# Decode kernel with two attention and two gated layers: the last normalisation from a scaled copy of x, rows of x by 32x32 transposition on VectorE, addition to x moved behind

## The chip, the core and the metric

One core of a Trainium2 chip runs the kernel. The metric is the device time of one execution in microseconds (us); three runs of the kernel before gave a median of 313.3 us. The core's engines are TensorE (PE, with its weight loads shown apart as PEld), VectorE (DVE), ScalarE (ACT), GpSimd (POOL) and SyncE (SP). Each takes its instructions in the order of the program; between engines they wait on semaphores.

## What is computed

Four rows of 512 numbers (one token for each of four sequences) pass through attention with a cache, a gated layer, the same attention again and the same gated layer again. Each of the four adds to x, and each starts with a normalisation of x.

```python
def _layernorm(x, axis=-1, eps=1e-5):
    m = jnp.mean(x, axis=axis, keepdims=True)
    v = jnp.var(x, axis=axis, keepdims=True)
    return (x - m) / jnp.sqrt(v + eps)
...
    def _A_ref(x, k_cache, v_cache, wq, wo):    # B=4, Sq=1, D=512, 32 heads, 8 kv heads, 4096 keys of 128
        q = (x @ wq).reshape(B, Sq, Hq, Dh).transpose(0, 2, 1, 3)
        scores = jnp.einsum("bhqd,bhkd->bhqk", q, k) * (Dh ** -0.5)
        p = _softmax(scores, axis=-1)
        o = jnp.einsum("bhqk,bhkd->bhqd", p, v)
        return o.transpose(0, 2, 1, 3).reshape(B, Sq, Hq * Dh) @ wo
...
    def _B_ref(x, w_gate, w_up, w_down):        # 512 -> 1792 -> 512
        g = jnp.einsum("bsd,df->bsf", x, w_gate)
        u = jnp.einsum("bsd,df->bsf", x, w_up)
        h = _sigmoid(g) * u
        return jnp.einsum("bsf,fd->bsd", h, w_down)
...
    x = x + _A_ref(_layernorm(x, axis=-1), A_k_cache, A_v_cache, A_wq, A_wo)
    x = x + _B_ref(_layernorm(x, axis=-1), B_w_gate, B_w_up, B_w_down)
    x = x + _A_ref(_layernorm(x, axis=-1), A_k_cache, A_v_cache, A_wq, A_wo)
    x = x + _B_ref(_layernorm(x, axis=-1), B_w_gate, B_w_up, B_w_down)
```

## The kernel before

Nearly all of the kernel is the two attention layers: 32 pairs of sequence and key-value head in each, whose keys and values stream from memory in 1 MB tiles and are worked on in an order written out by hand (`ORDER`, `LOADS`, `PROGRAM`). The change touches none of that. It touches the end, from line 1446 on: the last piece of attention's output projection, the last normalisation and the last gated layer.

The helper class `_Sched` keeps one list of instructions for each engine. `S.group`, `S.inst`, `dve(...)` and `act(...)` append to them in the order of the source; `reads` and `writes` are names of values, from which the waits follow, those between two instructions of one engine included. So the order of two statements in the source is the order of the queue when both go to one engine.

x lies transposed in `xT`: 128 partitions, 4 groups k of columns, 4 sequences b, so 16 numbers per partition. The end of the kernel before runs as follows; the line numbers are those of the profile.

- `do_wo` and `wo_units` (lines 1282 to 1321): the output projection of a head adds to `xT`: matmuls of line 1299 into a bank `O_ps`, then the addition on VectorE, line 1313. The last call of `do_wo` has a `then`, which is run between the two: `mean_of_last` (line 615).
- Mean: `mean_before` (605) sums x as it stands before the last addition, in two bf16 parts (`parts`, lines 588 and 589); `mean_of_last` (621) adds what the last addition will bring. Both sum into `M_ps[1]`.
- `ident_w` (1463, ScalarE) is a float32 identity, `eye4` (1465, VectorE) a small selection matrix made from it.
- `ln_a` (486): `xc_sb` = x minus mean (508, VectorE), `xc_bf`, its bf16 form times a constant (524, ScalarE), and the squares `sq_sb` (529, VectorE).
- Rows of x: eight float32 matmuls of line 1477 against `ident_w` turn `xT` into rows in bank `S_ps[1]` (the trace has them as 16), and line 1490 copies them to `x_row` (ScalarE). Row group c, at partitions 32c to 32c+3, holds the 128 columns c of x for the four sequences.
- `parts` splits the squares in two bf16 parts; `gate(0, 2)` issues the first 8 of the gate's 56 matmuls (744); `square_sums_of_parts` (634) sums the squares with two matmuls; `ln_b` (643) makes from them the reciprocal root `rs`, by nine small instructions on VectorE one after the other (648, 655, 660, then 558, 563, 569 twice); `gate(2, KF)` issues the other 48 matmuls, multiplies the gate by `rs` (757, VectorE) and takes the tanh (767, ScalarE).
- `sel_row` and `rowk_f` (1493, 1498, VectorE): `rs` as a scalar for each partition.
- `up_half(0)` and `up_half(1)`: 28 matmuls each (778), and on VectorE (788) the product with the gate, which gives the two halves of `hT_bf`.
- Down projection (1509): 56 matmuls in two groups; the first needs the first half of `hT_bf`, the second the second. Four go to four row groups of the bank at a time.
- Line 1522 (VectorE) multiplies by `rowk_f` and adds `x_row`; four DMAs (1531) write the four row groups out.

The order of TensorE's queue at the end is therefore 1299, 621, 1477, 744 (8), 634, 744 (48), 778 (28), 778 (28), 1509 (56).

Of the kernel before, what the change touches and what calls it, by code (L numbers as in the profile page):

```python
# [146 lines left out]
def bass_interleave_layers__gqa_block_cached__glu_gated_glu__decode_kernel(  # L147
# [17 lines left out]
    P = 128  # L165
# [98 lines left out]
    sq_sb = t_row[:, D // 2 + KD * Bn:D // 2 + 2 * KD * Bn].rearrange("p (k b) -> p k b", k=KD)  # L264
    ident_f = t_row[:, 0:P]
    half_f = t_row[:, P:P + 8 * REP].rearrange("p (u w) -> p u w", u=2)
    gs_sb = t_row[:, 0:KF * Bn]
    t_sb = t_row[:, 64:64 + KF * Bn]
    iota_f = pe_sb.rearrange("p j m -> p (j m)").bitcast(dt.float32)[:, 0:P]
# [213 lines left out]
    def bc(ap2, n, nb):  # L483
        return ap2.unsqueeze(1).broadcast_to([P, n, nb])
# [116 lines left out]
    def mean_before():  # L601
        S.group(
            "pe",
            [
                (lambda n, k: lambda e: e.matmul(
                    M_ps[1][:, 0:Bn], lhsT=ones_wb, rhs=sq_hl[:, n, k * Bn:(k + 1) * Bn],
                    start=(n == 0 and k == 0), stop=False,
                ))(n, k)
                for n in range(2) for k in range(KD)
            ],  # L610
            reads=["rb", "ones_b"],
            writes=["M1"],
        )

    def mean_of_last(us):
        u = seq[NU - 1][2]
        assert us == [u]
        S.last_write["M1"] = S.group(
            "pe",
            [  # L620
                (lambda n, r: lambda e: e.matmul(
                    M_ps[1][:, 0:Bn], lhsT=ws_hl[:, n, r:r + 1].broadcast_to([P, P]),
                    rhs=oT_sb[:, u * REP + r, 0:Bn], start=False, stop=(n == 1 and r == REP - 1),
                ))(n, r)
                for n in range(2) for r in range(REP)
            ],
            reads=["wsb"] + [f"oT_{u}_{c}" for c in range(Bn)],
        )
# [11 lines left out]
            writes=["M1"],  # L640
        )

    def ln_b(nb, sums=square_sums):
        M = M_ps[1]
        if sums is not None:
            sums(nb)
        dve(
            lambda e: e.tensor_reduce(
                lnsq[:, 0:nb], M[:, 32:32 + KD * nb].rearrange("p (k b) -> p b k", k=KD), AX.X, ALU.add
            ),  # L650
            reads=["M1"],
            writes=["nt_b"],
        )
        dve(
            lambda e: e.tensor_scalar(vpe[:, 0:nb], lnsq[:, 0:nb], inv_d, eps, op0=ALU.mult, op1=ALU.add),
            reads=["nt_b"],
            writes=["vpe"],
        )
        dve(
            lambda e: e.tensor_scalar(  # L660
                y0i[:, 0:nb], vpe[:, 0:nb].bitcast(dt.int32), -0.5, RSQRT_MAGIC, op0=ALU.mult, op1=ALU.add
            ),
            reads=["vpe"],
            writes=["y0i"],
        )
        y0 = y0i[:, 0:nb].bitcast(dt.float32)
        if nb == 1:
            newton_one(y0)
        else:
            newton_many(y0, nb)  # L670
# [552 lines left out]
    def normalise(g, uls=(0, 1)):  # L1223
        l, b, u = seq[2 * g]
        bank, key = out_of(g, uls[0])
        c = b if l == 1 else own_column
        u0, n = u + uls[0], len(uls)
        for ul in uls:
            assert not any(t[0] == l and t[2] == u + ul for t in ready)
            done.add((l, b, u + ul))  # L1230
            if l == 0 or all((1, bb, u + ul) in done for bb in range(Bn)):
                ready.append((l, b, u + ul))
        dve(
            lambda e: e.tensor_tensor(  # L1234
                oT_sb[:, u0 * REP:(u0 + n) * REP, c],
                bank[:, uls[0] * REP:(uls[0] + n) * REP],
                rden_sb[:, uls[0] * REP:(uls[0] + n) * REP],
                ALU.mult,
            ),
            reads=[key, "rden"],  # L1240
            writes=[f"oT_{u + ul}_{c}" for ul in uls],
        )
# [39 lines left out]
    def wo_units(us, l, b, p, then=None):  # L1282
        if l == 0:
            assert len(us) == 2
            if rows_in[b] < HKV // 2 - 1:
                wo_rows(us, b)
                return
            assert turning == [b, 3]
            turning.clear()
        bs = range(Bn) if l == 1 else [b]  # L1290
        cs = range(Bn) if l == 1 else [own_column]
        nb = len(bs)
        n = REP * len(us)
        out_w = O_ps[p][:, 64:64 + KD * nb]
        fns = []
        for c in range(KD):
            for r in range(n):
                fns.append(
                    (lambda c, r: lambda e: e.matmul(  # L1299
                        out_w[:, c * nb:(c + 1) * nb],  # L1300
                        lhsT=wo_sb[:, us[0] * REP + r, cols(c)],
                        rhs=oT_sb[:, us[0] * REP + r, cs[0]:cs[0] + nb],
                        start=(r == 0),
                        stop=(r == n - 1),
                    ))(c, r)
                )
        S.group(
            "pe", fns, reads=[f"oT_{u}_{c}" for u in us for c in cs] + [f"wo{u}" for u in us], writes=[f"O{p}"]
        )
        if then is not None:  # L1310
            then(us)
        dve(
            lambda e: e.tensor_tensor(
                xT[:, :, bs[0]:bs[0] + nb],
                xT[:, :, bs[0]:bs[0] + nb],
                out_w.rearrange("p (k b) -> p k b", k=KD),
                ALU.add,
            ),
            reads=[f"O{p}"],
            writes=[f"x{bb}" for bb in bs],  # L1320
        )

    def do_wo(p, then=None):
        if not ready:
            return False
        l, b, u = ready.pop(0)
        us = [u]
        if u % 2 == 0 and (l, b, u + 1) in ready:
            ready.remove((l, b, u + 1))
            us.append(u + 1)  # L1330
        wo_units(us, l, b, p, then)
        return True
# [114 lines left out]
        pass  # L1447
    parts(sq_hl, xT.rearrange("p k b -> p (k b)"), xkeys, "rb")
    mean_before()
    normalise(g, (1,))  # L1450
    do_wo((g + 1) % 2, mean_of_last)
    assert not ready
    free += spare
    assert not loads and len(free) == NSLOT + KD
# [1 line left out]
    home = free[0]  # L1456
    assert home not in free[-2:]
    ident_w = slot[home][:, 0:2 * P].bitcast(dt.float32)
    x_row = slot[home][:, 2 * P:4 * P].bitcast(dt.float32)
    eye4 = slot[home][:, 4 * P:4 * P + 2 * Bn].bitcast(dt.float32)  # L1460
    sel_row = slot[home][:, 4 * P + 16:4 * P + 16 + 2 * Bn].bitcast(dt.float32)
    o_row = slot[home][:, 5 * P:6 * P]
    act(lambda e: e.activation(ident_w, ident_bf[:, :], ACTF.Copy), reads=IDENT, writes=[f"s{home}"])
    dve(
        lambda e: e.tensor_reduce(
# [2 lines left out]
        reads=[f"s{home}"],  # L1468
        writes=["eye4"],
    )  # L1470

    ln_a(0, Bn, 0.5 * RS, M_ps[1][:, 0:Bn])
    fns = []
    for c in range(KD):
        for e_ in range(2):
            fns.append(
                (lambda c, e_: lambda e: e.matmul(
                    S_ps[1][32 * c:32 * c + Bn, bass.ds(e_, P // 2, step=2)],
                    lhsT=xT[:, c // 2 * 2 + e_, :],
                    rhs=ident_w[:, P // 2 * (c % 2):P // 2 * (c % 2 + 1)],  # L1480
                    start=True,
                    stop=True,
                ))(c, e_)
            )
    S.group("pe", fns, reads=xkeys + [f"s{home}"], writes=["S1"])
    parts(sq_hl, sq_sb.rearrange("p k b -> p (k b)"), ["rd"], "rb")
    gate(0, 2)
    square_sums_of_parts()
    ln_b(Bn, None)
    act(lambda e: e.activation(x_row, S_ps[1][:, 0:P], ACTF.Copy), reads=["S1"], writes=["x_row"])  # L1490
    gate(2, KF)
    dve(
        lambda e: e.tensor_tensor(sel_row, eye4, rs, ALU.mult),
        reads=["eye4", "rs"],
# [4 lines left out]
        reads=["sel_row"],  # L1499
        writes=["rowk"],  # L1500
    )
    up_half(0)
    up_half(1)
    for part in range(2):
        fns = []
        for k in range(KW * part, KW * part + KW):
            for c in range(KD):
                fns.append(
                    (lambda c, k: lambda e: e.matmul(
                        S_ps[0][32 * c:32 * c + Bn, 0:P],  # L1510
                        lhsT=hT_bf[:, k, :],
                        rhs=wd_sb[:, k, c * P:(c + 1) * P],
                        start=(k == 0),
                        stop=(k == KF - 1),
                    ))(c, k)
                )
        if part == 0:
            S.group("pe", fns, reads=["rc"] + wkeys["wd"], writes=["S0"])
        else:
            S.last_write["S0"] = S.group("pe", fns, reads=["rc", "rd"] + wkeys["wd"])  # L1520
# [8 lines left out]
        S.dma(  # L1529
            ("sp", "act")[c % 2],  # L1530
            (lambda c: lambda e: e.dma_start(
                out.rearrange("b s d -> (b s) d")[:, c * P:(c + 1) * P], o_row[32 * c:32 * c + Bn, :]
            ))(c),
            f"out{c}",
            reads=["o_row"],
# [47 lines left out]
```

## Time and profile before

| | us |
|---|---|
| median of three runs | 313.3 (312.93 to 313.76) |
| profiled execution, its time | 312.81 |
| span of its records | 310.6 |
| TensorE busy | 227.0 (73%) |
| VectorE busy | 179.8 (58%) |
| ScalarE busy | 106.8 (34%) |
| GpSimd busy | 40.4 (13%) |
| end of the last VectorE instruction (1522) | 308.31 |

The span is divided below into start times within it. The memory queues are busy to about the 296th microsecond; what lies behind is the tail that the change edits. In each stretch of that tail the profile has the same granted TensorE clock, 0.50 of full speed. A timeline line reads: start, time, engine, line, operation, what it writes and reads, its shape and how often; in square brackets the engine's idle time before it and what ended it.

### The profile page before, as it was taken

To read this page: it belongs to the slowest core of one execution; us is meant where nothing else is said; L and a number is where in the kernel's file an instruction comes from. 1 tells how busy PE (TensorE), PEld (TensorE's weight loads), DVE (VectorE), ACT (ScalarE), POOL (GpSimd) and SP (SyncE) were. 2 spreads that over 40 slices of the span, in tenths; PEclk is the share of its full clock that TensorE was granted. 3 is DMA by queue.
4 is the path that set the end of the run, shared out by engine and by line. 5 is a ranking of instruction groups with operands and counts; after the bars stand their busy time and mean duration, and the time that the engine had idled before them with its cause. 6 is when DMAs were issued, how large, how long until landed. Compare 5 with 4: busy or idle time off the path is not lost.

```text
span 310.6 us, 10146 instructions
## 1 busy us (share of the span) xinstructions
PE 227.0 (73%) x4306; PEld 138.5 (45%) x4306; DVE 179.8 (58%) x395; ACT 106.8 (34%) x351; POOL 40.4 (13%) x205
## 2 busy tenths in 40 slices
PE   1232366244889789799879898986768989789975
PEld 1220133032654354646444664544533754446765
DVE  6364757406334757587652468775565793894333
ACT  2010124204303365434234625236424313445600
POOL 0011110200000213011112011021101110212000
PEclk9999999999999855667755557575555575755555
DMA  7999999999999999999999999999999999999900
GB/s 290 417 424 411 407 422 378 390 406 419 407 415 418 413 379 415 426 418 418 419 390 386 424 421 420 421 419 419 420 414 424 400 358 401 424 422 420 407 27 5
DMA packets 20788, 120.45 MB, mean 388 GB/s; under 512 B 1924, under 2 KB 6024, under 8 KB 7688
## 3 DMA queue, kind: packets, MB, share of 16 engines
q1 hardware_dynamic: 20720, 119.81, 94.9%
q8 instruction: 34, 0.56, 0.7%
q14 instruction: 10, 0.08, 0.1%
q10 hardware_dynamic: 24, 0.01, 0.0%
HBM read 119.80 MB, written 0.00 MB: 386 GB/s over the span
## 4 chain that ended last, share of the span: by engine, by line
PE 26%; DMA 16%; DVE 9%; issue 4%; ACT 4%; POOL 1%; DVEq 0%; ACTq 0%; POOLq 0%; SPq 0%
DMA slot<-in_A_k_cache_dram 9%; PE O_ps L1203 8%; DMA slot<-in_A_v_cache_dram 7%; PE S_ps L1034 6%; DVE slot L1017 6%; PE PT L1105 3%; ACT pT L1157 3%; PE O_ps L1299 2%; PE M_ps L907 1%; POOL qz L731 1%; ACT pe L1083 1%; DVE small L1052 1%; PE O_ps L1060 1%; PE AC L1259 1%; PE M_ps L956 1%
## 5 line engine op out<-in xcount | busy, mean ns | idle before, releaser
L1017 DVE STREAM_TRANSPOSE slot<-slot 128x2048 f32<-128x2048 f32 (+1 forms) x50 | 101.5, 2040 | 24.5 <-DMA slot<-in_A_k_cache_dram 24.5
L1157 ACT ACTIVATE pT<-PT 32x128 bf16<-32x128 f32 x236 | 63.1, 267 | 58.6 <-PE PT L1105 38.6
L1034 PE MATMUL S_ps<-slot,qz 128*16 128x512 bf16 x496 | 56.6, 586 | 22.0 <-DVE slot L1017 10.9
L1203 PEld LDWEIGHTS O_ps<-pT,slot 128*128 128x128 bf16 x1856 | 54.8, 103 | 32.0 <-ACT pT L1157 19.2
L1203 PE MATMUL O_ps<-pT,slot 128*128 128x4 bf16 x1856 | 58.2, 166 | 12.3 <-ACT pT L1157 7.2
L1083 ACT ACTIVATE pe<-S_ps,small 128x512 bf16<-128x512 f32 x32 | 22.0, 687 | 71.6 <-DVE small L1071 41.2
L731 POOL COPY qz<-qs 32x32 bf16<-32x32 bf16 x128 | 26.0, 203 | 106.2 <-PE S_ps L1034 62.8
L1052 DVE TENSOR_REDUCE small<-S_ps 128x1 bf16<-128x512 f32 x32 | 21.9, 684 | 29.1 <-PE S_ps L1034 28.8
L1034 PEld LDWEIGHTS S_ps<-slot,qz 128*16 128x16 bf16 x496 | 10.6, 102 | 40.6 <-DVE slot L1017 13.2
L1105 PE MATMUL PT<-ident_bf,pe 128*128 128x64 bf16 (+1 forms) x288 | 27.7, 235 | 1.1 <-ACT pe L1083 1.0
L1105 PEld LDWEIGHTS PT<-ident_bf,pe 128*128 128x128 bf16 (+1 forms) x288 | 20.3, 123 | 13.6 <-ACT pe L1083 3.9
L1071 DVE CUSTOM_DVE_ANT_0 O_ps<-O_ps,small 128x64 f32<-128x64 f32 x32 | 9.0, 282 | 20.2 <-PE O_ps L1060 11.6
L1116 POOL CAST small<-small 128x1 bf16<-128x1 f32 x32 | 5.9, 186 | 99.7 <-ACT pe L1083 76.8
L1259 PE MATMUL AC<-wo,oT 128*1 128x512 bf16 x96 | 12.1, 617 | 7.5 <-DMA wo<-in_A_wo_dram 7.0
L907 PE MATMUL M_ps<-wq,small 128*1 128x512 bf16 x128 | 14.6, 604 | 0.0
L1060 PE MATMUL O_ps<-valid_p,small 128*128 128x64 bf16 x32 | 7.1, 223 | 8.5 <-DVE small L1052 8.5
L1234 DVE TENSOR_TENSOR oT<-O_ps,small 128x8 bf16<-128x8 f32 (+1 forms) x32 | 5.3, 164 | 13.3 <-PE O_ps L1203 12.6
L1060 PEld LDWEIGHTS O_ps<-valid_p,small 128*128 128x128 bf16 x32 | 3.3, 102 | 17.4 <-DVE small L1052 12.2
L1171 PE MATMUL O_ps<-small 128*128 128x8 bf16 x62 | 6.4, 174 | 4.9 <-DVE oT L1234 2.9
L1171 PEld LDWEIGHTS O_ps<-small 128*128 128x128 bf16 x62 | 4.0, 106 | 12.1 <-issue 6.5
L1299 PE MATMUL O_ps<-oT,wo 128*128 128x1 bf16 (+1 forms) x256 | 8.3, 166 | 0.9 <-DVE oT L1234 0.7
L716 ACT ACTIVATE qs<-M_ps 128x128 bf16<-128x128 f32 x8 | 1.9, 279 | 20.0 <-PE M_ps L705 20.0
(132 smaller groups left out, 198.4 us busy)
## 6 DMA issues: line engine op xcount, KB each, us to landing
slot<-in_A_v_cache_dram SPq DMA_DIRECT2D x52, 1024.0 KB, 11.3
slot<-in_A_k_cache_dram SPq DMA_DIRECT2D x44, 1024.0 KB, 12.1
wq<-in_A_wq_dram SPq DMA_DIRECT2D x2, 2048.0 KB, 10.2
wo<-in_A_wo_dram SPq DMA_DIRECT2D x8, 512.0 KB, 17.5
wq<-in_A_v_cache_dram SPq DMA_DIRECT2D x2, 1024.0 KB, 11.1
wq<-in_A_k_cache_dram SPq DMA_DIRECT2D x2, 1024.0 KB, 11.2
wg<-in_B_w_gate_dram SPq DMA_DIRECT2D x2, 896.0 KB, 16.0
wu<-in_B_w_up_dram SPq DMA_DIRECT2D x2, 896.0 KB, 22.3
```

What stands on the lines that cost most here:

```text
L731: (lambda a, ps: lambda e: e.tensor_copy(qz_sb[ps, :, :, a, :], qs_sb[b][ps, :, u * REP:(u + 2) * REP].rearrange("p t (u r) -> p u t r", r ...
L907: (lambda k, st: lambda e: e.matmul(M_ps[h][32 * st:32 * st + 1, :], lhsT=xc_bf[:, k, 0:1], rhs=wv[:, k, h, :, st, :], start=(k == 0), sto ...
L1017: dve(lambda e: e.transpose(kf, kf), writes=[f"s{st}"])
L1034: (lambda t, b2, e_, c, r0, ul: lambda e: e.matmul(S_ps[p][r0:r0 + 4 * REP, :], lhsT=qz_sb[:, ul, t, :, :].rearrange("p a r -> p (a r)"), ...
L1052: dve(lambda e: e.tensor_reduce(rm_bf, S_ps[p][:, :], AX.X, ALU.max), reads=[f"S{p}"], writes=["rmb"])
L1060: lambda e: e.matmul(O_ps[n][:, 128:128 + 16 * REP], lhsT=rm_bf.broadcast_to([P, P]), rhs=valid_p[:, :], start=True, stop=True,),
L1083: lambda e: e.activation(pe_sb.rearrange("p j m -> p (j m)"), S_ps[p][:, :], ACTF.Exp, bias=nm_sb, scale=exp_scale, accum_out=sm_sb,),
L1105: (lambda q0, q1, c0, m0, m1, a0, a1: lambda e: e.matmul(PT[q0:q1, c0:c0 + 16 * (a1 - a0)], lhsT=pe_flat[:, m0:m1], rhs=valid_bf[:, :, 4 * ...
L1157: (lambda dst, frm: lambda e: e.activation(dst, frm, ACTF.Copy))(dst, frm),
L1203: (lambda n, x, c, j: lambda e: e.matmul(bank[:, ul * REP:(ul + 1) * REP], lhsT=vv[:, x * JG + c * 4 + j, :], rhs=pT[:, x % 2, j, x // 2, ...
L1259: (lambda r, h, i: lambda e: e.matmul(AC[32 * r:32 * r + 1, :], lhsT=oT_sb[:, h, own_column:own_column + 1], rhs=wo_sb[:, h, :], start=(j ...
L1299: (lambda c, r: lambda e: e.matmul(out_w[:, c * nb:(c + 1) * nb], lhsT=wo_sb[:, us[0] * REP + r, cols(c)], rhs=oT_sb[:, us[0] * REP + r, c ...
```

## The change

- `mean_of_last` is replaced, as the `then` of the last `do_wo`, by a new function `last_norm`. It runs ahead of the last addition to `xT`. ScalarE has made `xm`, x times the constant `0.5 * RS`, ahead of it; `last_norm` adds the last projection from the bank times that constant (VectorE), then writes `xc_bf` and `xc_sb` from `xm` and the mean, both on VectorE, `xc_bf` first, then the squares and their parts. The addition to `xT` comes after that.
- `ln_a` is no longer called here. `ln_b` takes a factor for the scaled squares.
- The float32 matmuls of line 1477 and the copy of line 1490 go. Instead VectorE copies `xT` into `x_pad`, four groups of 32 columns of which four are filled, transposes it in 32x32 blocks, and makes `x_row` with two copies of 64 columns.
- `gate(0, 2)`, the sums of the squares, `ln_b` and `gate(2, KF)` now stand in the source ahead of `ident_w` and `eye4`.
- A row group now holds two runs of 64 columns instead of one of 128, so the down projection reads `wd_sb` in two runs, and each output DMA writes two runs of 64 for each sequence.

```diff
+    xm = t_row[:, D // 2 + 3 * KD * Bn:D // 2 + 4 * KD * Bn].rearrange("p (k b) -> p k b", k=KD)
...
+    def last_norm(us, out_w, p):
+        mean_of_last(us)
+        mult = 0.5 * RS
+        dve(
+            lambda e: e.scalar_tensor_tensor(
+                out=xm, in0=out_w.rearrange("p (k b) -> p k b", k=KD), scalar=mult, in1=xm,
+                op0=ALU.mult, op1=ALU.add,
+            ),
+            reads=[f"O{p}"],
+            writes=["xm"],
+        )
+        for dst, key in ((xc_bf, "xcb"), (xc_sb, "rc")):
+            dve(
+                (lambda dst: lambda e: e.scalar_tensor_tensor(
+                    out=dst, in0=bc(M_ps[1][:, 0:Bn], KD, Bn), scalar=-inv_d * mult, in1=xm,
+                    op0=ALU.mult, op1=ALU.add,
+                ))(dst),
+                reads=["M1", "xm"],
+                writes=[key],
+            )
+        dve(lambda e: e.tensor_tensor(sq_sb, xc_sb, xc_sb, ALU.mult), reads=["rc"], writes=["rd"])
+        parts(sq_hl, sq_sb.rearrange("p k b -> p (k b)"), ["rd"], "rb")
...
-    def ln_b(nb, sums=square_sums):
+    def ln_b(nb, sums=square_sums, inv_d=inv_d):
...
-            then(us)
+            then(us, out_w, p)
...
+    act(lambda e: e.activation(xm, xT, ACTF.Copy, scale=0.5 * RS), reads=xkeys, writes=["rc", "rd", "xm"])
     normalise(g, (1,))
-    do_wo((g + 1) % 2, mean_of_last)
+    do_wo((g + 1) % 2, last_norm)
...
-    x_row = slot[home][:, 2 * P:4 * P].bitcast(dt.float32)
+    x_pad = slot[home][:, 2 * P:4 * P].bitcast(dt.float32).rearrange("p (k w) -> p k w", k=KD)
+    x_row = slot[home][:, 6 * P:8 * P].bitcast(dt.float32)
...
+    gate(0, 2)
+    square_sums_of_parts()
+    ln_b(Bn, None, inv_d / (0.5 * RS) ** 2)
+    gate(2, KF)
     act(lambda e: e.activation(ident_w, ident_bf[:, :], ACTF.Copy), reads=IDENT, writes=[f"s{home}"])
     dve(
         lambda e: e.tensor_reduce(
...
-    ln_a(0, Bn, 0.5 * RS, M_ps[1][:, 0:Bn])
-    fns = []
-    for c in range(KD):
-        for e_ in range(2):
-            fns.append(
-                (lambda c, e_: lambda e: e.matmul(
-                    S_ps[1][32 * c:32 * c + Bn, bass.ds(e_, P // 2, step=2)],
-                    lhsT=xT[:, c // 2 * 2 + e_, :],
-                    rhs=ident_w[:, P // 2 * (c % 2):P // 2 * (c % 2 + 1)],
-                    start=True,
-                    stop=True,
-                ))(c, e_)
-            )
-    S.group("pe", fns, reads=xkeys + [f"s{home}"], writes=["S1"])
-    parts(sq_hl, sq_sb.rearrange("p k b -> p (k b)"), ["rd"], "rb")
-    gate(0, 2)
-    square_sums_of_parts()
-    ln_b(Bn, None)
-    act(lambda e: e.activation(x_row, S_ps[1][:, 0:P], ACTF.Copy), reads=["S1"], writes=["x_row"])
-    gate(2, KF)
...
+    dve(lambda e: e.tensor_copy(x_pad[:, :, 0:Bn], xT), reads=xkeys + [f"s{home}"], writes=["x_pad"])
+    dve(
+        lambda e: e.transpose(x_pad.rearrange("p k w -> p (k w)"), x_pad.rearrange("p k w -> p (k w)")),
+        writes=["x_pad"],
+    )
+    for h_ in range(2):
+        dve(
+            (lambda h_: lambda e: e.tensor_copy(
+                x_row.rearrange("p (h i e) -> p h i e", h=2, e=2)[:, h_, :, :],
+                x_pad.rearrange("p (h e) i -> p h i e", h=2)[:, h_, :, :],
+            ))(h_),
+            reads=["x_pad"],
+            writes=["x_row"],
+        )
     up_half(0)
     up_half(1)
...
-                        rhs=wd_sb[:, k, c * P:(c + 1) * P],
+                        rhs=wd_sb[:, k, :].rearrange("p (h a w) -> p h a w", h=2, a=KD)[:, :, c, :],
...
-                out.rearrange("b s d -> (b s) d")[:, c * P:(c + 1) * P], o_row[32 * c:32 * c + Bn, :]
+                out.rearrange("b s (h a w) -> a (b s) h w", h=2, a=KD)[c],
+                o_row[32 * c:32 * c + Bn, :].rearrange("p (h w) -> p h w", h=2),
```

## The prediction, made before any run of the change

> **What bounds the kernel now.** I read the page first: span 310.6 us, with the DMA row down from 9 tenths to 0 in the last two of its 40 slices. The change edits nothing ahead of the last projection, so what matters is which engine sets the end in the last 10 us. The chain of waits, for the stretch from 301 us (start, time, engine, what):
>
> ```profile
> 301.33 0.17 DVE small L1313
> ...
> 301.65 0.92 PE S_ps L1477 x16
> 302.57 0.31 PE M_ps L744 x8
> 302.88 0.06 PE M_ps L634 x2
> 302.94 1.27 PE M_ps L744 x48
> 304.21 0.75 PE M_ps L778 x28
> 304.95 0.72 PE O_ps L778 x27
> 305.68 0.37 issue
> 306.05 0.19 PE O_ps L778
> 306.23 1.62 PE S_ps L1509 x56
> ...
> 307.96 0.35 DVE slot L1522
> ```
>
> From 301.65 TensorE is the bound, back to back, but for one hole of 0.37 us at 305.68 that no semaphore explains ("issue"). The 0.92 us of the float32 turn (L1477) stands at its head, ahead of the gate. Next the timeline, for what VectorE and ScalarE do beside it:
>
> ```profile
> 295.02 0.31 ACT L1463 ACTIVATE slot<-ident_bf 128x128 f32<-128x128 bf16 x1
> ...
> 301.42 0.17 DVE L1465 TENSOR_REDUCE slot<-slot 128x4 f32<-128x16 f32 x1
> 301.55 0.17 DVE L508 SCALAR_TENSOR_TENSOR t_row<-M_ps,small 128x16 f32<-128x16 f32 x1
> ...
> 302.18 0.17 DVE L589 TENSOR_TENSOR t_row<-t_row 128x16 bf16<-128x16 f32 x1
> ...
> 302.97 0.17 DVE L648 TENSOR_REDUCE small<-M_ps 128x4 f32<-128x16 f32 x1 [0.62 <-PE M_ps L634]
> ...
> 304.78 0.22 DVE L757 TENSOR_TENSOR t_row<-M_ps,small 128x56 f32<-128x56 f32 x1
> ...
> 304.92 0.15 DVE L1493 TENSOR_TENSOR slot<-slot,small 128x4 f32<-128x4 f32 x1
> ...
> 305.03 0.25 ACT L767 ACTIVATE t_row<-t_row 128x56 f32<-128x56 f32 x1 [2.12 <-DVE t_row L757]
> 305.10 0.16 DVE L1498 TENSOR_REDUCE small<-slot 128x1 f32<-128x4 f32 x1
> 305.31 0.18 DVE L788 SCALAR_TENSOR_TENSOR t_row<-t_row,M_ps 128x28 bf16<-128x28 f32 x1
> ```
>
> VectorE runs a second chain close beside TensorE's: L648 to L757 without a pause, the tanh, and L788 at 305.31, only 0.85 us ahead of the down projection (306.16 in the timeline), which needs it. Two things can be read off as prices. An instruction that needs the one before it starts 0.03 to 0.04 us after its end (L1493 to L1498 0.18 with 0.15 busy; the root's steps 0.20 each with 0.16). One that doesn't need it overlaps it by 0.08 (L757 to L1493 0.14 with 0.22 busy; L1313 to L1465 0.09 with 0.17). And L1463, which feeds L1465, was done at 295, six us before anybody needed it.
>
> **The change, part by part.** *Head of the norm.* The scaled copy of x on ScalarE (216 ns by L524's row) runs from about 300.0, when L1313's addition before the last ends (299.95), and nothing stands behind it until the tanh: free; if it weren't, up to 0.2. Then on VectorE: `xm` at 301.33, where L1313 stood; `xc_bf` needs it and the mean, at 301.55 like L508 now; `xc_sb` overlaps it, 301.65; squares 301.86; parts 302.07 and 302.28; the moved addition to x (L1313) at 302.38, done 302.55, while TensorE sums the squares: free, and its first reader, the copy to `x_pad`, comes 3 us later. The last part thus comes 0.10 later than now (302.18).
>
> *TensorE's head.* With the turn gone (16 matmuls, 0.92 us) and `xc_bf` ready at 301.72, the gate starts at about 301.78 instead of 302.50. But only 8 of its matmuls stand ahead of the sums of the squares (L634), which must wait for the parts: from L589 to its reader takes 0.23 us (300.19 to 300.42 for L605), so L634 starts at 302.51 instead of 302.71, where it now queues behind turn and gate. The 0.72 us shrink to 0.20. L648 comes at 302.77, the steps up to L757 take 1.81 as now (302.97 to 304.78), L757 at 304.58; the other 48 gate matmuls are done at 302.71 + 1.27 = 303.98, in time. Tanh at 304.83, done 305.08.
>
> *ScalarE's queue.* `ident_w` (310 ns) used to run at 295.02. Its statement now stands behind `gate(2, KF)`, so it is queued behind the tanh. By L1157's rows one copy follows another 0.02 after its end; by L1083 the next instruction, its accumulator read, starts 0.11 ahead of it (292.64 against 292.06 + 0.69). Between the two I take 305.05 to 305.36.
>
> *VectorE's queue.* `eye4` waits for it, and stands, with six more, ahead of both L788. From 305.39 (0.03 after its end, as L788 after the tanh now): `eye4` +0.21, `sel_row` +0.18, `rowk_f` (the `x_pad` copy behind it is independent) +0.08, the copy of 128x16 (0.175 busy) +0.21, the transposition +0.35, two copies of 128x64, the second kept behind the first because both write `x_row`, +0.27 and +0.15 to L788, which doesn't need them. Sum 1.45: L788 starts at 306.84 and is done at 307.02. The unseen sizes: the transposition of 128x128 lies on the line through these rows, 212 + 96 x 1.03 = 311 ns:
>
> ```profile
> L1017 DVE STREAM_TRANSPOSE slot<-slot 128x1024 f32<-128x1024 f32 x12 | 14.8, 1236 | 1.4 <-DMA slot<-in_A_k_cache_dram 1.3
> L396 DVE STREAM_TRANSPOSE pe<-pe 128x32 f32<-128x32 f32 x1 | 0.2, 212 | 0.0
> ```
>
> The copies of 64 lie between 174 ns (L440, 32 columns) and 282 (L1071, 64 columns), nearest to L757's 56 columns at 217; I take 230. Bounds of this block: 1.0 (everything overlaps by 0.08, copies at 174) to 2.0 (nothing overlaps, copies at 282, transposition in place at the cost of two).
>
> At this place a page speaks against the change. The Trainium skill (VectorE: DVE Perf Modes, section Rules for kernel authors) says to save instructions on VectorE rather than semaphores, since each pays for its own emptying of the pipe, waited for or not. The trace agrees for dependent steps (0.20 each for 4 columns) and differs for independent ones (0.09 between starts). By the page's rule the three overlaps that I count on would go, some 0.3 us more.
>
> *Down projection.* It now waits for L788 and starts 0.06 later, at 307.08 instead of 306.16: +0.92. The second L788 follows 0.1 behind the first and isn't needed until 28 matmuls later. From its start to L1522 1.80 us as now (306.16 to 307.96). Reading two runs of 64 columns: no row has it, but L1034 reads strided columns at 586 ns for 512 and L907 contiguous ones at 604, so I take 0; bounds 0 and twice the 1.7. Output: twice as many pieces in each of four DMAs that are issued in 0.3 us each; I take 0.03, bounds 0 and 0.3.
>
> *Instruction supply.* From the end of a 1.30 us "issue" hole at 297.51 to the hole's end at 306.05 the timeline has 253 matmuls, each with a weight load; the page has 34 packets of instructions for 4306 matmuls, 127 for each. So each hole ends with a packet, and these came 4.27 us apart. With 16 matmuls fewer the edge that now lies at the last up matmul falls on the 16th of the down projection. There it is due at 306.1 to 306.3 and needed at 307.08 + 16 x 0.03 = 307.6: no hole. What the hole cost (0.37 on the present path) is already inside the difference of starts. The Trainium skill (Runtime: NRT & Kernel Launch, section Instruction fetch mechanics) calls the crossing of a block mostly hidden; here two crossings in the last 15 us show 1.30 and 0.37, so the trace differs, and by the page the hole would have another cause and stay where it is, under cover of VectorE's work: the sum is the same.
>
> **Sum.** L1522 moves from 307.96 to 308.88; with the DMAs +0.95. The profiled execution goes from 312.81 (span 310.6) to 313.76 (311.55). The median of the runs is 0.49 above that execution, so 314.2, 0.3% more. About 0.3%, 0.94 us, is what a measurement here can tell from no change: the forecast lies on that line.
>
> **Rivals.** *The row work on VectorE is hidden, not slower* (other side). TensorE alone would finish the up projection at 302.71 + 1.27 + 1.47 = 305.45, 0.8 earlier than now, then meet the packet edge at its 16th down matmul, due at about 306.2, and end at 306.2 + 41 x 0.029 = 307.4: L1522 at 307.5, 0.45 less, 312.9. It decides if L788 starts within 1.35 us of L757 (305.93; the down projection then starts at 306.16 as now). For it: VectorE's independent pitch of 0.09. Against it: `ident_w` and `eye4` alone take L788 to 305.65, and transposition and copies truly depend on one another.
>
> *The row work costs more.* Strided writes into `x_row`, the transposition over its own input, or no overlap: the block at 1.8 to 2.0 instead of 1.45, so 314.6 to 314.8, and 315 with a longer output. For it: nothing in the trace has these shapes. Against it: L1017 also transposes in place, on the same line.
>
> *The two runs of 64 slow the down projection*, by a half: +0.85 on top, 315.0. Only L1034's strided reads speak, and against it.
>
> **Chances.** Forecast 0.70 (313.7 to 314.7, of which somewhat under half over the line), hidden 0.07, dearer rows 0.17, down projection 0.06. Slower by over 0.3%: 0.30 + 0.17 + 0.05 = 0.52; faster 0.05; within 0.3% 0.43. Time of the likeliest 314.2. The range, 313.5 to 315.0, takes in the dearer rows and cuts the outer half of the two small cases.
>
> **What would show it.** Right: `ident_w` just behind the tanh near 305.1; `eye4` released by ScalarE; seven VectorE instructions between L757 and L788, 2.3 us between the starts of these two; TensorE idle 1.3 to 1.7 us ahead of the down projection with L788 as the releaser; L634 0.2 earlier than now and the gate's first 8 matmuls 0.7 earlier; no hole inside the down projection. Wrong: L788 under 1.4 us behind L757, a down projection longer than 1.8, a hole in it, or a move of anything ahead of 301 us.

## The result, and the profile after

The changed kernel takes 315.9 us (six runs, 314.96 to 316.28), the kernel before 313.48 beside it: ratio 1.0077, interval 1.0052 to 1.0101. A second comparison gave 1.0090 (1.0072 to 1.0108). It is slower, by about 2.3 us, and above the predicted range of 313.5 to 315.0.

The profiled execution took 315.89 us, its span 313.9. First the chain of waits of the changed kernel (start, time, engine, what); L781 is the product with `rs` (L757 before), L791 the tanh, L1493 and L1495 `ident_w` and `eye4`, L1513 the transposition, L1518 the copies to `x_row`, L629 `xc_bf` and `xc_sb`, L812 the product with the gate (L788 before), L1532 the down projection, L1545 the last VectorE instruction:

```profile
305.95 0.23 DVE t_row L781
306.18 0.02 issue
306.20 0.25 ACT t_row L791
306.45 0.21 ACT slot L1493
306.66 0.02 issue
306.69 0.19 DVE slot L1495
...
307.37 0.32 DVE slot L1513
307.69 0.02 issue
307.72 0.21 DVE slot L1518
307.94 0.20 DVE slot L1518
308.14 0.10 DVE t_row L812
308.24 0.04 issue
308.29 1.69 PE S_ps L1532 x29
...
310.08 0.35 DVE slot L1545
```

Where the chain before ran through TensorE's gate and up projections, it now runs through VectorE and ScalarE alone, from the tanh to the down projection. The timeline of the same profile shows who waited, and how the output starts:

```profile
303.18 0.38 PE L768 MATMUL M_ps<-small,wg 128*128 128x4 bf16 x8 [0.34 <-DVE small L629]
...
303.88 0.22 PE L658 MATMUL M_ps<-t_row,small 128*128 128x16 bf16 x2 [0.33 <-DVE t_row L590]
...
306.69 0.18 DVE L1495 TENSOR_REDUCE slot<-slot 128x4 f32<-128x16 f32 x1 [0.52 <-ACT slot L1493]
...
308.29 1.66 PE L1532 MATMUL S_ps<-wd,t_row 128*4 128x128 bf16 x56 [1.41 <-DVE t_row L812]
...
310.46 1.57 SPq L1554 DMA_DIRECT2D out_dram<-slot  x2
310.47 1.46 ACTq L1554 DMA_DIRECT2D out_dram<-slot  x2
```

TensorE stands idle for 1.41 us ahead of the down projection and is released by L812. And the two output DMAs of each queue now take 1.57 and 1.46 us to issue. In the profile before they took 0.67 and 0.62:

```profile
308.34 0.67 SPq L1531 DMA_DIRECT2D out_dram<-slot  x2
308.34 0.62 ACTq L1531 DMA_DIRECT2D out_dram<-slot  x2
```

The prediction had 0.03 us for this part. From the start of the last VectorE instruction to the end of the span it was 310.61 - 307.96 = 2.65 us, and is 313.88 - 310.08 = 3.80.

One thing in this pair is not the change's. The third addition to x counted from the end (the last but one that attention makes, line 1313 before and L1337 here) starts at 299.78 in the profile before and at 301.18 here, though the program up to it differs in nothing that lies on its way; the runs below show that this start scatters between executions. So the profiles are compared from that addition on: to the last VectorE instruction 8.18 before and 8.90 after, +0.72; the output +1.15.

### The profile page after: what moved, and what is told of

It reads as the page before. It is cut to its first block, busy times and chain, and to the rows that moved or that the text cites. A ratio compares the mean times of both kernels' runs of the same rounds, so it can differ in the third digit from the quotient of the medians.

```text
span 313.9 us, 10117 instructions
## 1 busy us (share of the span) xinstructions
PE 226.2 (72%) x4290; PEld 138.0 (44%) x4290; DVE 180.7 (58%) x401; ACT 106.5 (34%) x350; POOL 40.4 (13%) x205
## 4 chain that ended last, share of the span: by engine, by line
PE 29%; DMA 13%; DVE 9%; issue 4%; ACT 4%; POOL 1%; DVEq 0%; ACTq 0%; POOLq 0%; SPq 0%
DMA slot<-in_A_k_cache_dram 9%; PE O_ps L1227 8%; PE S_ps L1058 8%; DVE slot L1041 5%; DMA slot<-in_A_v_cache_dram 4%; PE PT L1129 3%; ACT pT L1181 3%; PE M_ps L931 2%; PE O_ps L1323 2%; ACT pe L1107 1%; POOL qz L755 1%; PE O_ps L1084 1%; DVE small L1076 1%; PE AC L1283 1%; PE M_ps L860 1%
## 5 line engine op out<-in xcount | busy, mean ns | idle before, releaser
L885 PE MATMUL M_ps<-wu,small 128*1 128x512 bf16 (+1 forms) x64 | 8.9, 538 | 0.0
```

## The experiments

Each is compared with the kernel before on the same chip. A table of what the profiles gave comes after them. "The third addition" is the one named above, and "the last VectorE instruction" is meant by its start.

**Output DMAs alone, undone in the changed kernel.** Its output DMAs write one run for each sequence:

```diff
-                out.rearrange("b s (h a w) -> a (b s) h w", h=2, a=KD)[c],
-                o_row[32 * c:32 * c + Bn, :].rearrange("p (h w) -> p h w", h=2),
+                out.rearrange("b s d -> (b s) d")[:, c * P:(c + 1) * P], o_row[32 * c:32 * c + Bn, :]
```

> The changed kernel, but each output DMA writes one run of 128 columns for each sequence, as before the change (so the output's columns stand at other places). Theory 1 (the two runs make the DMAs dearer): the first VectorE instruction of the end (L1545) to the end of the span shrinks from 3.8 to about 2.65 us, the four issues from 0.64 to 0.84 each to about 0.3; time about 314.7, 1.2 under the changed kernel. Rival (the output is late for another reason, such as the queues' state): it stays 3.8, and 315.9. For the start of the third addition to x before the end (299.8 in the profile before, 301.2 after): if the 1.4 there belong to the change it is near 301.2; if they are scatter between executions it can be anything from 299.5 to 301.5.

Measured 314.05 us (12 runs), ratio 1.0031 (1.0015 to 1.0046). The output is back to 312.04 - 309.41 = 2.63. Its two DMAs on SyncE (min, median, max in ns):

```profile
L1554 SPq DMA_DIRECT2D out_dram<-slot x2: 338/341/344, 309.8 to 310.2; - x2
```

**Output DMAs alone, done in the kernel before** (the same diff the other way round).

> The kernel before, but each output DMA writes two runs of 64 columns for each sequence (so the output's columns stand at other places). Theory 1: L1522 to the end of the span grows from 2.65 to about 3.8 us, ratio to before about 1.004 (314.7). Rival: no change, ratio 1.000. Ahead of the output it is the kernel before to the letter: the third addition to x before the end near 299.8 if that time belongs to the program, scattered over 1 us or more if not.

Measured 314.65 us (10 runs), ratio 1.0048 (1.0028 to 1.0068). The output grows to 312.76 - 308.96 = 3.80, and the issues are those of the changed kernel:

```profile
L1531 SPq DMA_DIRECT2D out_dram<-slot x2: 684/762/841, 309.3 to 310.2; - x2
```

Undone and done agree: two runs per sequence cost 1.15 to 1.17 us in the span, with either program ahead of them. Of this, 0.85 to 0.90 lie in SyncE's two issues (1.57 in all against 0.72 and 0.67), and 0.25 to 0.32 between the end of the last issue and the end of the span. The third addition came at 301.06 in a program that is the kernel before up to its output, so its place is scatter.

**`ident_w` and `eye4` early.** The two statements go ahead of `gate(0, 2)`:

```diff
+    act(lambda e: e.activation(ident_w, ident_bf[:, :], ACTF.Copy), reads=IDENT, writes=[f"s{home}"])
+    dve(... eye4 ...)
     gate(0, 2)
     square_sums_of_parts()
     ln_b(Bn, None, inv_d / (0.5 * RS) ** 2)
     gate(2, KF)
-    act(lambda e: e.activation(ident_w, ident_bf[:, :], ACTF.Copy), reads=IDENT, writes=[f"s{home}"])
-    dve(... eye4 ...)
```

> The changed kernel with ident_w and eye4 ahead of the gate, as before the change. Theory 1 (0.8 us of the way from the gate's product to the down projection is the wait for ident_w behind the tanh): the first product with the gate (L812) starts 1.3 us behind L781 instead of 2.10, and the time is 315.1. Rival (the chain of row instructions alone sets it): 2.0, and 315.8.

Measured 314.41 us (8 runs), ratio 1.0039 (1.0021 to 1.0057). Its timeline:

```profile
305.09 0.22 DVE L781 TENSOR_TENSOR t_row<-M_ps,small 128x56 f32<-128x56 f32 x1
...
306.37 0.18 DVE L812 SCALAR_TENSOR_TENSOR t_row<-t_row,M_ps 128x28 bf16<-128x28 f32 x1
...
306.60 1.67 PE L1532 MATMUL S_ps<-wd,t_row 128*4 128x128 bf16 x56 [0.59 <-DVE t_row L812]
```

L812 is 1.28 behind L781 instead of 2.10; TensorE's idle time shrinks from 1.41 to 0.59. The queueing of `ident_w` behind the tanh was worth 0.82 us in the profile. The time is 0.7 under the 315.1 expected, as was that of the run with one-run output under its 314.7; both had been counted down from the 315.9 of the first comparison.

**Rows last.** As in the last run, and the four row instructions behind both products:

```diff
-    dve(lambda e: e.tensor_copy(x_pad[:, :, 0:Bn], xT), ...)   # and the transposition, two copies
     up_half(0)
     up_half(1)
+    dve(lambda e: e.tensor_copy(x_pad[:, :, 0:Bn], xT), ...)   # and the transposition, two copies
```

> As the run with ident_w and eye4 early, and the four row instructions (copy to x_pad, transposition, two copies to x_row) behind both products with the gate on VectorE. Theory 1 (row work ahead of the products is the whole loss ahead of the output): the product starts 0.5 behind L781, the down projection when the up projection ends, about 0.8 behind L781 instead of 2.34, and the time is 314.4; the rows are done before the down projection is. Rival (TensorE's instruction supply stops it at the 16th down matmul): a hole of 0.3 to 0.6 there, 314.8.

Measured 314.53 us (7 runs), ratio 1.0043 (1.0027 to 1.0059). The chain of waits of this profile is TensorE's from the gate to the end:

```profile
304.94 0.75 PE M_ps L802 x28
305.69 0.75 PE O_ps L802 x28
306.44 1.62 PE S_ps L1532 x56
```

No hole at the 16th down matmul. The way from the third addition to the last VectorE instruction, 7.42, is 0.66 shorter than with `ident_w` early alone, but the time was not shorter. Hence a second run of it:

> The kernel with the rows last once more. Its profile made it 7.42 from the third addition to the last VectorE instruction, which with the dearer output gives 313.8; its runs gave 314.5. If TensorE's instruction supply stops it at the 16th down matmul in some executions, this profile may show a hole there; if it was scatter ahead of the end, the ratio comes out near 1.0015.

Measured 314.06 us (12 runs), ratio 1.0027 (1.0012 to 1.0041), 7.42 again and no hole again. The 313.8 expected counted from the first profile of the kernel before, whose way was lengthened by its own hole. Counted from its other two profiles (below), which have none, this program is 11.22 - 10.30 = 0.92 longer from the third addition to the end of the span, so about 314.3, and the two medians lie 0.3 above and 0.3 below that. No hole at the 16th down matmul is needed to explain them, and neither profile has one.

**The two kernels once more.**

> The kernel before once more, for a second profile. The third addition to x before the end came at 299.78 in its first profile and between 300.3 and 301.2 in the five profiles since, that of the same program with other output DMAs included (301.06). If that is scatter, it lands near 300.5 here and from there to the end of the span it is 10.83 again; if the kernel before is really earlier there, 299.8. Ratio 1.000 with an interval that tells what this comparison can resolve.

> The kernel before under a label of its own, beside the next one. The last comparison of this kind gave 1.0018 for a kernel against itself; 1.000 to 1.002 again. Its profile gives a third value for the hole at the last up matmul, which was 0.37 in the first and absent in the second: third addition to L1522 between 7.6 and 8.2.

The kernel before under its own label came to 314.01 us (12 runs), ratio 1.0018 (1.0000 to 1.0037), and to 313.38 (12 runs), ratio 0.9997 (0.9977 to 1.0017): 0.2% is what a comparison here can be off. Its second profile, chain of waits:

```profile
305.07 0.75 PE M_ps L778 x28
305.81 0.75 PE O_ps L778 x28
306.56 1.62 PE S_ps L1509 x56
```

The hole of 0.37 us at the last up matmul, on which the prediction's base stood, is not there, nor in the third profile; both take 7.65 from the third addition to L1522 where the first took 8.18, and 10.30 to the end of the span, not the 10.83 expected.

> The changed kernel once more. By the end of the profiles alone (third addition to the last VectorE instruction 8.90 against 8.18, output 3.8 against 2.65) it should be 1.9 over before, ratio 1.006; the first comparison gave 1.0077. If what lies ahead of the third addition (1.4 between the first two profiles) belongs to the change, the ratio is 1.010 and the addition comes at 301.2 again.

Measured 315.68 us (6 runs), ratio 1.0090 (1.0072 to 1.0108). The profile has 8.90 and 3.80 once more, but the third addition at 299.51, earlier than in any profile of the kernel before. So what lay ahead of it in the first pair is put down to scatter.

**Eight DMAs of one run.**

```diff
-        for c in range(KD)
+        for c in range(KD) for h in range(2)
...
-                out.rearrange("b s (h a w) -> a (b s) h w", h=2, a=KD)[c],
-                o_row[32 * c:32 * c + Bn, :].rearrange("p (h w) -> p h w", h=2),
+                out.rearrange("b s (h a w) -> h a (b s) w", h=2, a=KD)[h, c],
+                o_row[32 * c:32 * c + Bn, 64 * h:64 * h + 64],
```

> The changed kernel with eight output DMAs of one run of 64 columns each instead of four of two runs. If the dearness is the pieces as such, the output (last VectorE instruction to the end of the span) is again 3.8 us. If it is the pattern of two runs per sequence (0.64 to 0.84 per issue against 0.3), each of the eight issues takes 0.3 and the output about 2.65 + 2 x 0.33 = 3.3, 0.5 under the changed kernel.

Measured 315.13 us (12 runs), ratio 1.0057 (1.0034 to 1.0080); the output took 313.76 - 310.40 = 3.36. SyncE's issues in this profile:

```profile
L1554 SPq DMA_DIRECT2D out_dram<-slot x4: 298/320/346, 310.8 to 311.9; - x4
```

That is near the 3.3 expected if two runs in one DMA are what is dear, and 0.44 under the changed kernel with the same pieces. But it is 0.73 over the 2.63 of the four DMAs of one run, which have half as many pieces. Two issues with one run of 128 bytes for each sequence take 2 x 0.32, one with two such runs 0.64 to 0.84, one with a run of 256 bytes 0.27 to 0.35. Whether the time to issue goes by the number of pieces, or by the DMA with an extra for a second run, these runs do not tell apart; it does not go by the bytes, which are 4 KB in all.

**A version without either loss.** `ident_w` and `eye4` early, the copy to `x_pad` and the transposition between the two products, and `x_row` by eight copies that put 128 columns of x in one run again, so that the down projection and output are those of before:

```diff
+    up_half(0)
     dve(lambda e: e.tensor_copy(x_pad[:, :, 0:Bn], xT), ...)
     dve(lambda e: e.transpose(...), writes=["x_pad"])
-    for h_ in range(2): ...
-    up_half(0)
     up_half(1)
+    for c in range(KD):
+        for u in range(2):
+            a = 2 * (c % 2) + u
+            dst = x_row4[32 * c:32 * c + 32, u, :, :]
+            frm = x_pad.rearrange("p (h e) i -> p h i e", h=2)[32 * a:32 * a + 32, c // 2, :, :]
+            # u == 0 on VectorE, u == 1 on ScalarE
```

> The changed kernel with ident_w and eye4 early, the copy to x_pad and the transposition between the two products with the gate, and x_row made by eight copies of 32 partitions by 64 columns (four on VectorE, four on ScalarE) so that a row group holds 128 columns in one run again: the down projection and the output DMAs are those of before. If the account holds (row work ahead of the products and two-run DMAs are the loss), third addition to the last VectorE instruction takes 7.4 us against 8.18 before, the output 2.65, and the time is about 0.7 under before, ratio 0.998. If the down projection now waits for TensorE's instructions at its 16th matmul in most executions (which would explain why the run with the rows last came out at 314.5 and not 313.8), 313.4, ratio 1.000, and a hole in its profile.

> The version with the row work spread behind the first product and contiguous output once more. Its first profile: third addition to the last VectorE instruction 7.46, output 2.64, against 7.65 to 8.18 and 2.65 before; the gain by profiles is 0.2 to 0.7 (0.998 to 0.999), its first ratio 1.0004 (0.9986 to 1.0022). It should come out 0.2 to 0.7 below the kernel before under its own label; if it doesn't, the gain is below what this comparison can show.

Measured 313.17 us, ratio 1.0004 (0.9986 to 1.0022), and 312.80, ratio 0.9985 (0.9963 to 1.0007), 12 runs each. By profile it is 0.2 shorter than the kernel before without its hole and 0.7 shorter than with it. The loss is gone as far as the comparisons can tell; that this version beats the kernel before is not shown, since both intervals hold 1.

| profile | third addition at | from it to the last VectorE instruction | from that instruction to the end of the span |
|---|---|---|---|
| before, first | 299.78 | 8.18 | 2.65 |
| before, second and third | 300.64, 300.93 | 7.65, 7.65 | 2.65, 2.66 |
| before, two-run output | 301.06 | 7.90 | 3.80 |
| after, first and second | 301.18, 299.51 | 8.90, 8.90 | 3.80, 3.80 |
| after, one-run output | 300.50 | 8.91 | 2.63 |
| after, eight DMAs | 301.49 | 8.91 | 3.36 |
| after, `ident_w` early | 300.32 | 8.08 | 3.80 |
| after, rows last (two) | 300.74, 300.73 | 7.42, 7.42 | 3.80, 3.79 |
| neither loss (two) | 300.80, 300.85 | 7.46, 7.45 | 2.64, 2.64 |

The last two columns repeat to 0.01 for one program, but for the hole at the last up matmul, which only programs with the tail of the kernel before show: where it is 0.37 us the way is 8.18 instead of 7.65, and where it is 0.11, in the profile with two-run output, 7.90. All else that differs between the spans of one program in these profiles lies ahead of the third addition. The granted TensorE clock in the tail is 0.50 in every one of them.

Taken against 10.30 us, the kernel before without its hole, the way from the third addition to the end of the span agrees with the measured ratio to within 0.5 us in all ten comparisons of edited programs. Against 10.83, with the hole, all ten come out longer than the profiles make them, by 0.2 to 1.0 us.

## Why the prediction missed

*Head of the norm: right.* The gate's first matmuls came when `xc_bf` was written, and then TensorE waited 0.33 us for the parts (L658, above). From the third addition to the product with `rs` it took 305.95 - 301.18 = 4.77, against 304.78 - 299.78 = 5.00 before: 0.23 gained, 0.20 predicted.

*ScalarE's and VectorE's queues: right.* From that product to the product with the gate 2.26 were predicted and 2.10 measured, 0.16 less; `ident_w` began 0.16 behind the tanh's start, a little more overlapped than taken. The transposition took 0.31, as read off the line through the two rows. The part that a page would have added (the Trainium skill, VectorE: DVE Perf Modes, Rules for kernel authors, no gain from a missing wait) did not come: the copy to `x_pad` started 0.07 behind `rowk_f`, which it doesn't need and which took 0.16. The run with `ident_w` early shows what waiting for it cost, 0.82; the run with the rows last shows another 0.66 for the row work ahead of the product. Less the 0.23 gained at the head, that is the 1.25 us by which the changed kernel's way to the last VectorE instruction is longer than that of the kernel before without its hole.

*Down projection: right.* 1.79 from its start to the last VectorE instruction, 1.80 predicted; two runs of 64 columns cost TensorE nothing. The rival that they would is out.

*The output: the step that failed.* "Output: twice as many pieces in each of four DMAs that are issued in 0.3 us each; I take 0.03, bounds 0 and 0.3." It costs 1.15 to 1.17, shown by doing and by undoing it alone. The prediction takes the issue time of 0.3 us as nearly unmoved by the second run and names no row for its 0.03 or for its bounds. The two issues in a row on each queue carry most of the cost: each grew from 0.28 to 0.35 us to 0.64 to 0.84. The first profile had the price of a DMA with one run in four partitions and none with two; nothing in it excluded a doubling, and a doubling of four issues, two behind each other, is 0.6 to 0.7 alone.

*The base of the sum: half a microsecond off where the hole is absent, as in two of three profiles and, to judge by the times, in most executions.* "at 307.08 instead of 306.16: +0.92" takes from the kernel before a start that the hole had delayed. Two more profiles of it have no hole and make the way 7.65, so against them the change loses 8.90 - 7.65 = 1.25 ahead of the output, not 0.72. The prediction had said that the hole was inside the difference; it took for a part of the program what comes and goes.

*The sum.* 1.25 and 1.15 are 2.4 in the span; what lies outside it was 2.1 to 2.2 before and 2.0 after, so some 2.2 us, or 1.7 where the hole occurs. Measured 2.42 and 2.26 by the medians, ratios with 0.2% of slack. Of the rivals, the dearer rows and the hidden row work did not occur. The direction was right, by two terms that were each sized too small. One of them, the output, was in no rival as the thing that decides; with the +0.92 left as predicted, its 1.15 alone makes 315.4, out of the range.

## What to carry to other kernels

When data are laid out anew near the end, follow the new layout up to the last DMA: here the way it was issued cost 1.15 us where the new head of the norm saved 0.23. A statement that moves behind another in the source moves in every queue that it feeds, and here an operand that had been ready for six microseconds became the one waited for. Before a tail is summed up from one profile, see which of its idle times have a releaser; one without may be gone in the next execution.

## What the runs showed of the hardware that was not expected

A DMA of 1 KB from four partitions took 0.27 to 0.35 us to issue with one run of 256 bytes in each, and 0.64 to 0.84 with two runs of 128 bytes; DMAs with one run of 128 bytes in each took 0.27 to 0.35 too.

The idle times without a releaser on TensorE differ between executions of one program: the one near 297 us lasted 1.11 to 1.95 in the timelines of the thirteen profiles, the one at the last up matmul 0.37 in one profile of the kernel before, 0.11 in that with two-run output and nothing in two others. The Trainium skill (Runtime: NRT & Kernel Launch, section Instruction fetch mechanics) has the crossing of a block of instructions mostly hidden; the second of these agrees with it in two profiles of four, the first does not, with over a microsecond in each. That these idle times are waits for instructions was read off their spacing, not tested; by the prediction's own count (253 matmuls, 127 to a packet) a third crossing lies between the two, near L1477, where the matmuls stood idle for no more than 0.21 us, with a releaser.

The profiles hold one more sign. In those four, the packet on the instruction queue q8 that started 2.3 to 2.9 us ahead of the last up matmul took 1.39 us (2.9% of 16 engines in a window of 3 us) where the idle time was 0.37, 1.20 where it was 0.11, and 1.06 and 1.01 where there was none. This fits a wait for instructions that arrive late in some executions; no run changed it to find out.
